# The first group's triangular inverse: substitution on blocks of 16 rows, joined to 32 on TensorE

## The chip, the cores and the metric

One NeuronCore of one Trainium2 chip runs the whole kernel. The metric is the device time of one launch in microseconds (us), the median of several launches. Of each kernel one launch was also taken with the profiler, and all views below come from such launches. All launches quoted were in the fast state: none took over 1.5% more than the fastest of its kernel. A record is one matmul (with its weight load) as the trace lists it; a small fp32 product of the program comes as two of them. A view numbers the lines of the kernel that it was taken from, so the same code has another L number before and after.

## The reference, cut to what matters

```python
def _attn_ref(q, k, v, beta):            # 4 batches x 8 heads, 768 steps, head_dim 48
    k_n = k / (np.linalg.norm(k, axis=-1, keepdims=True) + 1e-06)
    state = np.zeros((B, H, D, D)); y = np.zeros_like(q)
    for t in range(S):
        y[:, :, t] = q_t @ state
        state += beta_t * outer(k_t, v_t - state^T k_t)
def _moe_ref(x, w_gate, w_val, w_out):   # 3072 tokens, 384 -> 1536 -> 384
    g = x @ w_gate
    return (g * sigmoid(g) * (x @ w_val)) @ w_out
# reference: _moe_ref on the attention's y, reshaped to (3072, 384); all fp32 results,
# the weights arrive as 64-bit floats
```

The kernel computes the recurrence in 12 chunks of 64 steps. For each chunk and head it needs the inverse of a 64 x 64 unit triangular matrix. Chunks are inverted in groups of two. The inverses of a group's 32-row diagonal blocks are found by substitution on VectorE, for all heads at once, and TensorE joins two of them to 64 rows. Then come the products of the recurrence (called p_r, p_u, p_s, p_y below), the transposition p_f, and for each chunk the FFN (gate and value products in twelve column tiles, taken in pairs, then the output products p_o).

## The kernel before

The substitution on 32 rows works on all 128 partitions, one 32-row block each, in 31 steps of two instructions:

```python
def substitute(mb, zb):
    for j in range(R - 1):                      # R = 32
        m = R - 1 - j
        ...
        nc.vector.tensor_tensor(out=t_v, in0=zb[:, 0:j+1, j:j+1]..., in1=mb[:, j:j+1, j+1:R]..., op=ALU.mult)
        nc.vector.tensor_tensor(out=zb[:, 0:j+1, j+1:R], in0=zb[...], in1=t_v, op=ALU.add)
```

The start of the program (cut): chunk 0 is joined before the first gate product; chunk 1's join is put behind gate pairs that are already running.

```python
for n, _ in enumerate(substitute(mb, zb)):
    ...                                   # 24 us on VectorE
m_1 = turned_m(1, "ffn")                  # second group's matrix, turned on TensorE meanwhile
...
first_join = join_late(0, 0, ("px", "py"))
next(first_join); converts(2); next(first_q); next(first_join)
step("advance", advance, 0); converts(2)  # chunk 0's recurrence between weight conversions
...
second = join_late(0, 1, ("ffn", "py"))   # chunk 1: handed to the gate loop
first.extend((state_and_join, second_join, lambda: gram(1, True)))
pairs = [(c, f) for c in range(2) for f in range(0, 8, 2)]
```

`converts(n)` turns n pieces of the 64-bit weights into fp32 on VectorE (with some help of ScalarE). `fill` is called in every gate pair and gives VectorE one or two more pieces while there are any, then steps of the second group's inverse.

Of the kernel before, what the change touches and what calls it, by code (L numbers as in the profile page):

```python
# [14 lines left out]
C = 64  # L15
DP = 64
R = 32
PIECE = 512


@with_exitstack
def kernel(
# [8 lines left out]
    moe_w_out: bass.AP,  # L31
    out: bass.AP,
):



# [88 lines left out]
    def load_q(c):  # L125
        for bp in range(NB):
            for b in range(2):
                nc.sync.dma_start(
                    out=qpad[c % QB][64 * b : 64 * b + 64, bp, :, 0:D],
                    in_=halves(q, c, bp, b).rearrange("h p d -> p h d"),  # L130
                )
# [54 lines left out]
    N_HALF = sum(piece[4] < PIECE for piece in pieces)  # L186
    for t in range(FT):
        pieces.append((wo_sb, moe_w_out, t, 0, DM))
    assert DFF == 1536 and KT == 3 and DM <= PIECE and 2 * HH * C == 4 * PIECE

    staged, powers, places = {}, {}, {}

    def words(tile_):
        return tile_.bitcast(U32)
# [30 lines left out]
    def stage(n):  # L225
# [10 lines left out]
            out=place, in_=src[t * 128 : (t + 1) * 128, f0 : f0 + m].bitcast(U32)  # L236
        )

    def power_step(n):
        if n in powers or n not in staged:  # L240
            return
        m = pieces[n][4]
        power = words(hp[10 + (n // 2 % 4 if n < N_HALF else (0, 2, 3, 1)[n % 4])])
        power = power[:, n % 2 * m : n % 2 * m + m] if n < N_HALF else power[:, 0:m]
        powers[n] = power
        nc.vector.tensor_scalar(  # L246
            out=power,
            in0=staged[n][:, :, 1],
            scalar1=0x7FF00000,
            scalar2=None,  # L250
            op0=ALU.bitwise_and,
        )

        nc.scalar.activation(  # L254
            power.bitcast(I32), power, ACTF.Relu, bias=rebias, scale=8.0
        )

    def convert(ns):

        work_of = []  # L260
        for n in ns:
            dst, _, t, f0, m = pieces[n]
            power_step(n)
            work_of.append((dst[:, t, f0 : f0 + m], staged.pop(n), powers.pop(n)))
        for dst, words, _ in work_of:
            nc.vector.tensor_scalar(
                out=dst.bitcast(U32),
                in0=words[:, :, 1],
                scalar1=0xFFFFF,
                scalar2=1 << 20,  # L270
                op0=ALU.bitwise_and,
                op1=ALU.bitwise_or,
            )
        for dst, words, _ in work_of:
            nc.vector.scalar_tensor_tensor(
                out=dst,
                in0=words[:, :, 0],
                scalar=2.0**-32,
                in1=dst.bitcast(U32),
                op0=ALU.mult,  # L280
                op1=ALU.add,
            )
        for n in range(ns[-1] + 1, ns[-1] + 7):
            if n < min(N_HALF, len(pieces)) or ns[-1] + 3 > n < len(pieces):
                power_step(n)
        for _, words, power in work_of:
            nc.vector.scalar_tensor_tensor(
                out=power,
                in0=words[:, :, 1],
                scalar=0x80000000,  # L290
                in1=power,
                op0=ALU.bitwise_and,
                op1=ALU.bitwise_or,
            )
        for dst, _, power in work_of:
            nc.vector.scalar_tensor_tensor(
                out=dst,
                in0=dst,
                scalar=2.0**-20,
                in1=power.bitcast(FP32),  # L300
                op0=ALU.mult,
                op1=ALU.mult,
            )
        for n in ns:
            for later in freed_by.get(n, ()):
                stage(later)
# [10 lines left out]
    for b in range(2):  # L317
        rows = mask_q[64 * b : 64 * b + 64]
        nc.gpsimd.affine_select(
            out=rows,  # L320
            in_=rows,
            compare_op=ALU.is_ge,
            fill=0.0,
            base=-1,
            pattern=[[1, C]],
            channel_multiplier=-1,
        )

    state = const.tile([128, 2, NB, NJ, D], FP32, name="state")
    kt, qt, a_sb, a_of, p_sb, xts = {}, {}, {}, {}, {}, {}  # L330
# [3 lines left out]
    def half_of(x):  # L334
        return slice(64 * x, 64 * x + 64)
# [102 lines left out]
    def gram_steps(c, of_q, tag=None, copies=(nc.vector.tensor_copy,) * 2):  # L438
# [10 lines left out]
        if of_q:  # L449
            p_sb[c] = work.tile([128, 2, NB, NJ, C], FP32, name="p_sb", bufs=2)  # L450
        elif c % 2 == 0:
            a = work.tile([128, C * 2 * HH], FP32, name="a_sb")

            a_sb[c // 2] = (
                a.rearrange("p (i c h) -> p c h i", c=2, h=HH)
                if c == 0
                else a.rearrange("p (c h i) -> p c h i", c=2, h=HH)
            )
            a_of[c // 2] = a
        yield  # L460
        for par in range(2):
# [13 lines left out]
    def gram(*args):  # L475
        for _ in gram_steps(*args):
            pass
# [32 lines left out]
    def substitute(mb, zb):  # L510
        for j in range(R - 1):
# [14 lines left out]
            )  # L526
            yield

    def recur(p, m=D):
        p = p[:, :, 0 : NB * NJ * m]  # L530
        return p.rearrange("p x (bp j d) -> p x bp j d", bp=NB, j=NJ)

    QUADS = [(slice(R * n, R * n + R), R * (n % 2)) for n in range(4)]
    z_late = {}

    def turned_m(g, tag):
# [256 lines left out]
    def gate_val(c, f, fill, within=None):  # L793

        ps = {}
        for w_sb, name in ((wg_sb, "p_gate"), (wv_sb, "p_val")):
# [10 lines left out]
            if name == "p_gate":  # L807
# [3 lines left out]
                if within is not None:  # L811
                    point(within)
        at = len(hs) if c < 2 else (len(hs) - 12) % 8
        hs[c, f] = hp[at].rearrange("p (i n) -> p i n", i=2)
        nc.vector.tensor_tensor(out=hs[c, f], in0=sil, in1=ps["p_val"], op=ALU.mult)  # L815
        if c >= FAST:
# [270 lines left out]
    with tc.manual_schedule(  # L1087
# [13 lines left out]

        nc.vector.memset(places[0][:, 0:1], 0)
        norms(1)
        for n in range(4):
            stage(n)
        load_q(0)
        load_k(2)
        load_k(3)
        for n in range(4, 10):
            stage(n)  # L1110
        load_v(0)
        load_q(1)
        stage(10)
        stage(11)
        copy_a, copy_v = nc.scalar.copy, nc.vector.tensor_copy
        turned(0, False)
        turned(1, False, "py")
        gram(0, False)
        gram(1, False, "py", (copy_a, copy_v))
        mb = new_mb()  # L1120
        a_v = a_of[0].rearrange("p (i m) -> p i m", i=C)
        for _ in turn(
            lambda rows, half: mb[rows],
            lambda rows, half: a_v[rows, R * half : R * half + R],
        ):
            pass
        r_b = first_n()
        copy_v(beta_b, beta_s.rearrange("p (g r) -> p g r", g=NG)[:, :, 0:R])
        for n in range(12, 17):
            stage(n)  # L1130
        load_v(1)
        divide_beta(0, r_b)
        zb = scale_m(mb, [(slice(0, R), mb)], beta_b[:, 0])
        nc.gpsimd.memset(ztp[0], 0.0)

        turned(0, True, "ffn")
        turned(2, False, "px")
        turned(3, False, "py")
        first_q = gram_steps(0, True, "ffn")
        next(first_q)  # L1140
        gram(2, False, "px", (copy_a, copy_a))
        gram(3, False, "py", (copy_a, copy_a))
        for n, _ in enumerate(substitute(mb, zb)):
            if n == R // 2:
                for i in range(4):
                    power_step(i)
        m_1 = turned_m(1, "ffn")
        scale_v_heads(0)
        turned(1, True, "px")
        for _ in late_z(0, zb):  # L1150
            pass
        mb = new_mb()
        mbs.append(mb)
        first_join = join_late(0, 0, ("px", "py"))
        next(first_join)
        converts(2)
        next(first_q)
        next(first_join)
        nc.scalar.copy(mb[:, m_1[0][0]], m_1[0][1])
        step("advance", advance, 0)  # L1160
        converts(2)
        step("advance", advance, 0)
        nc.scalar.copy(mb[:, m_1[1][0]], m_1[1][1])
        converts(2)
        step("advance", advance, 0)
        converts(2)
        step("advance", advance, 0)
        converts(2)
        second_inverse.append(invert(1))
        for _ in range(2):  # L1170
            next(second_inverse[0])
        second = join_late(0, 1, ("ffn", "py"))
        converts(2)

        def state_and_join():
            step("advance", advance, 0)
            next(second)

        def second_join():
            next(second)  # L1180
            gens["join", (0,)] = [None, 2]

        first.extend((state_and_join, second_join, lambda: gram(1, True)))


        pairs = [(c, f) for c in range(2) for f in range(0, 8, 2)]
        pairs += [(c, f) for f in range(8, FT, 2) for c in range(2)]
        for c, f in pairs:
            early = c == 0 and f < 8
            if c == 1 and f == 0:  # L1190
                finish(1)
            elif f > 0:
                point(1 if early else 2)
            need((6, 12, 18, 18, 24, 24)[f // 2])
            gate_val(c, f, fill, 1 if early else None)
# [53 lines left out]
```

## Time and profile before

Times of the kernel before in this study: 748.54 us median beside the changed kernel (747.8 to 749.3 in the other batches). I divide the span at three moments that each trace shows: T, the first gate product; V, the end of the last value product of chunks 0 and 1; G, the first gate product of chunk 2.

The windows view of the kernel before, cut at T, V and G. Columns: start and end, length, busy time and count of TensorE, of weight load, VectorE, ScalarE, GpSimd, then granted clock, DMA share and GB/s.

```profile
0.00:67.57 67.57, 34.41 (x951) 28.94 (x951) 56.56 (x150) 27.81 (x66) 21.49 (x29) 0.71 0.67 159
67.57:155.66 88.09, 87.38 (x1150) 75.74 (x1151) 75.31 (x157) 33.77 (x58) 16.50 (x6) 0.95 0.42 110
155.66:200.58 44.92, 44.23 (x679) 29.19 (x678) 36.41 (x76) 8.48 (x16) 7.34 (x3) 1.00 0.18 33
200.58:748.40 547.82, 540.64 (x7226) 480.23 (x7226) 306.92 (x599) 79.49 (x139) 22.04 (x9) 1.00 0.17 28
```

Length minus TensorE's busy time is its idle time: 33.2 us before T, then only 0.7, 0.7 and 7.2 us. What makes T earlier pays, as long as nothing is added behind it.

From the timeline of TensorE before G: recurrent products of chunk 2 stand between output products (p_o).

```profile
188.12 1.15 PE L695 MATMUL p_r<-state,kt 64*64 64x48 f32 x64
190.26 1.56 PE L829 MATMUL p_o<-wo_sb,h_f 128*128 128x384 f32 x4
...
200.58 2.86 PE L800 MATMUL p_gate<-x_ffn,wg_sb 128*128 128x256 f32 x12 [0.61 <-ACT x_ffn L783]
```

The reader is to see that a set of 64 small records takes 1.15 us here, at full clock, and that large products lie between the sets.

The page's line of the engines and of the queue that brings instructions (packets, MB, share):

```profile
PE 706.7 (94%) x10004; PEld 614.1 (82%) x10004; DVE 475.2 (63%) x981; ACT 149.5 (20%) x277; POOL 67.4 (9%) x46
...
q8 instruction: 78, 1.28, 0.7%
```

It looks like nothing: 0.7%. It turns out to matter, and the prediction did not read it.

### The profile page before, as it was taken

How to read it: one execution, taken by the hardware profiler on the slowest of the kernel's cores; microseconds unless marked ns; L12 is line 12 of the kernel's file. 1: busy time of each engine (PE TensorE's matmuls, PEld its weight loads, DVE VectorE, ACT ScalarE, POOL GpSimd, SP SyncE). 2: the span in 40 equal slices, each digit the busy share in tenths (PEclk: the TensorE clock that was granted, in tenths of full speed). 3: DMA queues.
4: the chain of work that ended last, by engine and by line, in shares of the span. 5: the costliest groups of instructions: out<-in, count | busy, mean ns of one | idle time of the engine just before them, and what ended most of it. 6: DMA issues, size and time to landing. Idle time of an engine off the chain costs nothing.

```text
span 748.4 us, 22217 instructions
## 1 busy us (share of the span) xinstructions
PE 706.7 (94%) x10004; PEld 614.1 (82%) x10004; DVE 475.2 (63%) x981; ACT 149.5 (20%) x277; POOL 67.4 (9%) x46
## 2 busy tenths in 40 slices
PE   4647999999999999999999999999999999999997
PEld 3536888866788688988888988988988988989987
DVE  5899888979368453478863478863478854223122
ACT  2346434211311111112011112011112011021010
POOL 7106200200300000030000030000030000000000
PEclk9755999999999999999999999999999999999999
DMA  7774534230203002231300331401220200000000
GB/s 154 184 213 109 148 68 124 64 53 23 55 14 50 16 16 32 47 61 34 54 14 17 49 61 28 57 10 24 42 46 2 43 3 3 22 3 0 22 1 21
DMA packets 130734, 37.17 MB, mean 50 GB/s; under 512 B 122864, under 2 KB 125936, under 8 KB 130640
## 3 DMA queue, kind: packets, MB, share of 16 engines
q1 hardware_dynamic: 127184, 34.01, 22.4%
q10 hardware_dynamic: 3072, 1.57, 1.0%
q8 instruction: 78, 1.28, 0.7%
q0 software_dynamic: 384, 0.17, 0.2%
q14 instruction: 16, 0.13, 0.1%
HBM read 31.01 MB, written 4.72 MB: 48 GB/s over the span
## 4 chain that ended last, share of the span: by engine, by line
PE 84%; DVE 10%; DMA 1%; issue 1%; SPq 1%; ACT 1%; ACTq 0%; DVEq 0%
PE p_gate L800 24%; PE p_val L800 23%; PE p_o L912 15%; PE p_o L829 6%; DVE tmp L515 3%; DVE zb L521 3%; PE p_g L444 2%; PE p_j L580 2%; PE p_y L735 2%; PE p_u L716 2%; PE p_s L747 2%; PE p_r L695 1%; PE p_y L704 1%; DVE h_f L870 1%; SPq L120 1%
## 5 line engine op out<-in xcount | busy, mean ns | idle before, releaser
L800 PE MATMUL p_gate<-x_ffn,wg_sb 128*128 128x256 f32 x864 | 208.3, 392 | 1.6 <-ACT x_ffn L783 1.6
L800 PE MATMUL p_val<-x_ffn,wv_sb 128*128 128x256 f32 x864 | 198.5, 379 | 0.0
L800 PEld LDWEIGHTS p_gate<-x_ffn,wg_sb 128*128 128x128 f32 x864 | 163.8, 194 | 25.4 <-ACT x_ffn L783 2.1
L800 PEld LDWEIGHTS p_val<-x_ffn,wv_sb 128*128 128x128 f32 x864 | 163.8, 190 | 22.3
L815 DVE TENSOR_TENSOR h_f<-sil,p_val 128x512 f32<-128x512 f32 x71 | 48.5, 684 | 152.4 <-PE p_val L800 151.9
L809 ACT ACTIVATE sil<-p_gate 128x512 f32<-128x512 f32 x72 | 43.0, 598 | 281.7 <-PE p_gate L800 258.1
L608 POOL TENSOR_TENSOR n_b<-mb,half 128x32 f32<-128x32 f32 x5 | 42.2, 8435 | 411.1 <-DVE mb L485 373.3
L912 PE MATMUL p_o<-wo_sb,h_f 128*128 128x192 f32 x432 | 75.6, 328 | 0.1
L515 DVE TENSOR_TENSOR tmp<-zb,mb 128x31 f32<-128x31 f32 (+15 forms) x186 | 63.2, 340 | 16.2 <-PE p_j L580 10.9
L912 PEld LDWEIGHTS p_o<-wo_sb,h_f 128*128 128x128 f32 x432 | 70.3, 190 | 1.2 <-DVE o_sb L922 0.7
L521 DVE TENSOR_TENSOR zb<-zb,tmp 128x31 f32<-128x31 f32 (+15 forms) x186 | 63.7, 342 | 6.4
L922 DVE TENSOR_TENSOR o_sb<-o_sb,p_o 128x192 f32<-128x192 f32 x45 | 15.7, 350 | 53.7 <-PE p_o L912 36.5
L829 PE MATMUL p_o<-wo_sb,h_f 128*128 128x384 f32 x136 | 45.7, 490 | 0.0
L829 PEld LDWEIGHTS p_o<-wo_sb,h_f 128*128 128x128 f32 x136 | 25.4, 190 | 16.5
L912 PE MATMUL p_o<-last_k,h_f 128*128 128x192 f32 x180 | 32.2, 326 | 0.0
L912 PEld LDWEIGHTS p_o<-last_k,h_f 128*128 128x128 f32 x180 | 29.7, 190 | 0.0
L870 DVE TENSOR_TENSOR h_f<-h_f,h_f 128x256 f32<-128x256 f32 x54 | 22.4, 424 | 8.0 <-PE p_o L912 7.1
L912 PE MATMUL p_o<-last_h,h_f 128*128 128x192 f32 x144 | 26.3, 326 | 0.0
L912 PEld LDWEIGHTS p_o<-last_h,h_f 128*128 128x128 f32 x144 | 23.9, 190 | 0.0
L254 ACT ACTIVATE last_h<-last_h,rebias 128x512 int32<-128x512 uint32 (+2 forms) x26 | 15.3, 616 | 31.8 <-DVE last_h L246 31.8
L485 DVE STREAM_TRANSPOSE mb<-a_sb 32x1024 f32<-32x1024 f32 x10 | 19.5, 1949 | 0.3
L716 PEld LDWEIGHTS p_u<-vin,zt 64*64 64x64 f32 x768 | 13.4, 141 | 6.1 <-issue 3.2
(163 smaller groups left out, 677.1 us busy)
## 6 DMA issues: line engine op xcount, KB each, us to landing
vin<-in_v_dram SPq DMA_DIRECT2D x96, 48.0 KB
kn<-in_k_dram SPq DMA_DIRECT2D x40, 96.0 KB
out_dram<-o_sb SPq DMA_DIRECT2D x36, 96.0 KB
zt<-in_moe_w_out_dram SPq DMA_DIRECT2D x6, 384.0 KB
staged<-in_moe_w_out_dram SPq DMA_DIRECT2D x6, 384.0 KB
qpad<-in_q_dram SPq DMA_DIRECT2D x36, 64.0 KB
wo_sb<-in_moe_w_gate_dram SPq DMA_DIRECT2D x4, 512.0 KB
wo_sb<-in_moe_w_val_dram SPq DMA_DIRECT2D x4, 512.0 KB
```

Of the source, the lines that this page charges most:

```text
L485: nc.vector.transpose(out(rows, 0), in_(rows, 0))
L515: nc.vector.tensor_tensor(out=t_v, in0=zb[:, 0 : j + 1, j : j + 1].to_broadcast([128, j + 1, m]), in1=mb[:, j : j + 1, j + 1 : R].to_broad ...
L521: nc.vector.tensor_tensor(out=zb[:, 0 : j + 1, j + 1 : R], in0=zb[:, 0 : j + 1, j + 1 : R], in1=t_v, op=ALU.add,)
L608: nc.gpsimd.tensor_tensor(out=n, in0=mb.rearrange("p j i -> p (j i)")[:, 0 : R * R : R + 1], in1=half, op=ALU.pow,)
L716: nc.tensor.matmul(p_u[half_of(b), par, bp, j], zt[half_of(b ^ par), par, bp, j], r[half_of(b ^ par), par, bp, j], start=first, stop=True, ...
L800: nc.tensor.matmul(ps[name][:, i], w_sb[:, t, (f + i) * 128 : (f + i + 1) * 128], xts[c][:, t], start=(t == 0), stop=(t == KT - 1),)
L809: nc.scalar.activation(sil, ps[name], ACTF.Silu)
L815: nc.vector.tensor_tensor(out=hs[c, f], in0=sil, in1=ps["p_val"], op=ALU.mult)
L829: nc.tensor.matmul(p_o, hs[c, f - f % 2][:, f % 2, bp * 128 : (bp + 1) * 128], wo_sb[:, f], start=(f == 0), stop=(f == FT - 1),)
L870: nc.vector.tensor_tensor(out=out, in0=a, in1=b, op=ALU.subtract)
L912: nc.tensor.matmul(p[x, part], a(f - f % 2)[:, f % 2], b(f), start=not begun and f == 0, stop=f == FH - 1, skip_group_check=True,)
L922: nc.vector.tensor_tensor(out=out, in0=a, in1=b, op=ALU.add)
```

## The change

Its intent is to shorten the 24 us of substitution, in which TensorE mostly waits. Only the first group is changed. The two 16-row diagonal halves of each 32-row block are substituted side by side in one partition (15 steps instead of 31), from grams computed as blocks of their own; the off-diagonal 16 x 16 part follows by products on TensorE. Core of the diff, cut:

```diff
+    def first_gram(c, tag, copies):           # 64 products per chunk, 64x32 tiles
+            nc.tensor.matmul(p_v[hi, par, 1, h], k_v[:, 0], k_v[:, 0])
+            nc.tensor.matmul(p_v[lo, par, :, h], k_v[:, 1], k_v)
+    def first_substitute(m, z):               # RH = 16: two blocks to a partition
+        for j in range(RH - 1):
+            ...
+    def first_m_z(c):                         # 64 products on four quadrants
+                nc.tensor.matmul(p[quad, h], fg.m_up[quad, h], fg.d[quad, :, HH * c + h])
+    def first_rest(p): ...                    # VectorE: identity minus that
+    def first_zt(c, p, blk): ...              # 32 products on two quadrants, twice
+    def first_z(c, p): ...                    # 32 products
+    def first_m_zt(c, p): ...                 # the join to 64 rows: 32 products
+    def first_last(p, t2): ...                # and 32 more
-        for n, _ in enumerate(substitute(mb, zb)):
+        for n, _ in enumerate(first_substitute(m, z)):
-        first_join = join_late(0, 0, ("px", "py"))
...
+        first_turned()
+        p_mz = first_m_z(0)
+        first_rest(p_mz)
+        first_zt(0, p_z[:, 0], 1)
+        first_to(0, p_z[:, 0], both, 1, R)    # copies, ScalarE and VectorE
+        first_zt(0, p_z[:, 0], 0)
+        first_z(0, p_z[:, 1])
+        ...                                   # the same for chunk 1, all ahead of the first gate
-        second = join_late(0, 1, ("ffn", "py"))
-        pairs = [(c, f) for c in range(2) for f in range(0, 8, 2)]
+        pairs = [(c, f + i) for f in (0, 4) for c in range(2) for i in (0, 2)]
         for c, f in pairs:
-            early = c == 0 and f < 8
+            early = c == 0 and f < 4
             if c == 1 and f == 0:
                 finish(1)
+                first.extend((lambda: second_gram(2), lambda: second_gram(3), second_m))
```

So the second group's grams and the turning of its matrix (p_m, 256 records) also leave the head and go into the FFN. The loads of v, q and weights are issued in another order.

## The prediction

> **What bounds the kernel now.** I read the windows by stage first (where TensorE is idle and at what clock), then the timeline of the first 110 us, then the waits of TensorE. The windows, with busy time of TensorE, weight load, VectorE, ScalarE, GpSimd, then the clock:
>
> ```profile
> 0.00:23.63 23.63, 12.83 (x168) 9.79 (x168) 14.79 (x25) 6.90 (x11) 15.35 (x28) 0.93 0.78 157
> 23.63:47.74 24.11, 9.65 (x459) 8.48 (x456) 21.94 (x66) 9.48 (x28) 0.52 (x1) 0.66 0.81 231
> 47.74:67.57 19.83, 11.94 (x327) 10.66 (x327) 19.83 (x59) 11.43 (x27) 5.62 (x1) 0.50 0.36 74
> 67.57:108.25 40.68, 39.97 (x743) 34.08 (x744) 35.17 (x67) 17.59 (x29) 11.73 (x1) 0.90 0.48 128
> 108.25:748.40 640.15, 632.28 (x8312) 551.09 (x8311) 383.47 (x765) 104.15 (x183) 34.16 (x17) 1.00 0.18 33
> ```
>
> The reader is to see a head of 67.57 us in which TensorE is not the bound, and 681 us in which it is busy 98 to 99%. So a gain is an earlier first FFN product, provided no new holes open behind it. In the head VectorE substitutes for 24.1 us (23.63 to 47.74), then 19.8 us of joins and chunk 0 follow. The timeline shows the pieces I use:
>
> ```profile
> 23.63 0.19 DVE L515 TENSOR_TENSOR tmp<-zb,mb 128x31 f32<-128x31 f32 x1
> 34.84 0.42 DVE L515 TENSOR_TENSOR tmp<-zb,mb 128x256 f32<-128x256 f32 x1
> 47.42 0.21 DVE L521 TENSOR_TENSOR zb<-zb,tmp 128x31 f32<-128x31 f32 x1
> 33.52 2.07 PE L544 MATMUL p_m<-ident,a_sb 32*32 32x32 f32 x128 [0.54 <-issue]
> 61.05 1.96 PE L735 MATMUL p_y<-uu,p_sb 64*64 64x48 f32 x64 [0.69 <-ACT uu L727]
> 67.57 5.28 PE L800 MATMUL p_gate<-x_ffn,wg_sb 128*128 128x256 f32 x12 [0.95 <-ACT x_ffn L783]
> 73.86 2.00 PE L568 MATMUL p_j<-zt,a_sb 32*32 32x32 f32 x64
> 182.88 2.00 PE L580 MATMUL p_j<-ident,d_t 32*32 32x32 f32 x64
> 180.26 1.20 PE L568 MATMUL p_j<-zt,a_sb 32*32 32x32 f32 x64
> ```
>
> A substitution step costs 0.19 us for 31 elements and 0.42 for 256; start to start it fits 0.195 us + elements/960 us per instruction. A small product comes as two records. On two quadrants with a strided operand a record takes 31 ns (2.00/64), on four 16 ns (2.07/128), on two with both operands contiguous 19 ns (1.20/64). The first gate product takes 5.28 us, later ones 2.59 start to start. The second thing to see is that VectorE is nearly full too from 47.7 to 108 (55.0 of 60.5 us): it converts weights, 2.8 us for two pieces of 256 columns, 2.5 us for one of 512. TensorE hardly waits because 12 pieces are done when its first product starts.
>
> **What the Trainium skill says.** "TensorE: Matmul & The Clock Gate", section "What's actually happening": the array's clock is halved by default and only sustained activity releases it. The trace agrees: 0.50 in the third window, 5.28 against 2.59 us. "TensorEngine Tiling (Array Packing)", section "Key Properties": tiles load and multiply independently; agrees (31 ns on two quadrants, 16 on four). "SBUF — State Buffer", section "Door 1: The DMA port swizzle", note on cachelines: reading a new 16-byte line for each element costs extra. The trace agrees for the stationary operand: L580 (stride of 32 floats) takes 2.00 us also at full clock, L568 falls to 1.20 when group 1 stores its operand contiguously. That a strided moving operand is as slow no row here shows; I assume it.
>
> **The change, part by part.**
>
> Start of the substitution. The first grams become 64 products per chunk instead of 32. Before, 128 records took 3.69 us; now 256, by dispatch (16 ns) 4.1 us, by the row halves up to 6.8: end at about 16 us. Copies of half size 0.6, norm, reciprocal and transposition 0.8, one transposition 1.27 in place of three (1.25 + 2.48), scaling 0.95 with half the elements: start at about 19.8 instead of 23.63.
>
> Substitution. 15 steps of two instructions, elements 2(j+1)(15-j), together 1360 per instruction kind: 30 x 0.195 + 2 x 1360/960 = 8.7 us, and two exponent steps 0.4: 9.1 instead of 24.1. End S at 28.9 instead of 47.7, 18.8 us earlier.
>
> Joins. What follows is now a chain on TensorE. From S: transposition 1.2; 64 products on four quadrants 2.07 (to 3.4); subtraction 0.7 (4.2); three sets of 32 products on two quadrants, 31 ns x 192 = 5.95 (10.2); the next product set on contiguous operands about 1.4, its copy 0.6, then a ScalarE copy of the upper part 0.4 that stands in the way of chunk 1's first 64 products (2.07): 14.8; chunk 0's last set 1.4; chunk 1's first set 2.0; p_u 2.0 (half clock, as p_y's 1.96), then, in TensorE's order ahead of p_y, two more sets 4.0; p_y 2.0; six copies of y 1.96; p_f 1.55; eight transpositions of q 1.95; and the last set 1.4, which waits for ScalarE's copies behind x_ffn. With 0.05 to 0.15 us per handover this adds to 33.3 us, where the old kernel needs 19.8, because both chunks' joins now lie ahead of the first gate. First gate T at 28.9 + 33.3 = 62.2 instead of 67.57: gain 5.4 us of the 18.8.
>
> Behind the first gate. VectorE has converted only 6 pieces at T (old: 10 to 12), as it waited for the joins. The new order of pairs (chunk 0, columns 0 and 2, then chunk 1) needs 12 pieces, and needs chunk 1's attention after two pairs, not four. From the order of instructions: piece 7 waits for ScalarE until T + 1.7; then VectorE stands until the first value product ends at T + 5.3 + 1.1 + 2.6 = T + 9; then product 0.7, pieces 9 and 10 2.4, mask 1.35, pieces 11 and 12 with exponents 4.35, pieces 13 and 14 4.9, and only then the two operations on v (2.05): p_u starts at T + 24.8. TensorE has nothing between the second value product (ends T + 19) and p_u: a hole of about 6 us. After it p_u, copy 0.85, p_s and p_y, copies 1.45, p_f, copy 0.8 run with no gates between them: 7.2 us at full clock, 10.4 at half; mean 8.8, gate of chunk 1 at T + 33.6. The old kernel takes 40.7 from T to that gate, with two more pairs (10.4) and a join (1.93 + 3.75 = 5.7) in it, so 24.6 for the same work: loss 9.0.
>
> Moved TensorE work: in the FFN -5.7 (join), +2.2 (grams of chunks 2, 3), +4.1 (256 records of p_m): +0.6. Clock: the gate after p_m at half clock +1.6 (old: 4.19 us after the join at 206, for 2.59), the gate after the hole +1.5.
>
> End of the first two chunks. The second inverse is emitted wholly after the last gate pair, and its join and chunk 2 stand in one block after all output products, where the old kernel has them between. The inverse itself (about 31 us) is covered by the 33 us of output products. But t, zt copies (2.34), p_r, p_u, uu, p_y, y, p_f run serially: about 49 us from last value product to the next gate at full clock, 53 at half, against 46.8 for the old (44.8, plus 2.0 for a transposition and a gram done earlier there): loss 2 to 6, say 4.
>
> Sum: -5.4 + 9.0 + 0.6 + 3.1 + 4 = +11.3 us. The clock terms (3.1, 1.6 in the mean of the advance, 2 in the last) may be absent; counting half of them takes off 3.3. Result 747.7 + 8 = about 756 us.
>
> **The rivals.**
> 1. The gain of the head is kept. The substitution falls by 15 us, and TensorE bounds all the rest; if small sets run at 19 ns, not 31 (strided moving operand not slow), four sets lose 0.8 each, T is at 59, and if the holes are covered too, the time is 738 to 742. For it: TensorE waits only 1.6 us for x_ffn in the whole trace. Against it: VectorE's 55 of 60.5 us, the instruction order.
> 2. VectorE becomes the bound behind the gate, as above, but the clock also stays at half through the joins of p_m and of the second group: 762 to 767.
> 3. Transfers: weights and v are issued in another order, v ahead of most weights. Pieces 2 to 8 are issued by about 30 us and needed after 49; the DMA share of 0.36 in the third window speaks against a wait. 0 us. If beta landed only near 20 us, the substitution would start some 2 us later.
>
> **Range and chances.** Head: T 59 to 65 (3 us either way); hole and serial chunk 1: 5 to 11; end 0 to 8; clock 0 to 4. Combined: 741 to 767. Faster by over 2% is below 732.7, which needs the whole head saving and no loss: 0.05. Slower by over 2% is above 762.7: 0.18. Within: 0.77.
>
> **What would show it.** Substitution about 9 us long, ending near 29; first gate at 59 to 65 at half clock; TensorE idle about 6 us before chunk 1's p_u with VectorE at weights; 64-record sets at 2 us; the second join after all output products. It is wrong if VectorE delivers v before the second value product ends, if the first gate lies before 55, or if no hole over 2 us shows between 62 and 100 us.

## The result, and the profile after

The changed kernel took 775.53 us (774.69 to 778.79, 4 launches); the kernel before, in the same rounds, 748.54. The ratio is 1.0373, interval 1.0333 to 1.0413. It is slower by 3.7%, above the predicted range. Ratios here are the mean time of one kernel's fast runs over that of the other's of the same rounds, so not quite the ratio of the medians.

The windows of the changed kernel, cut at the start and end of the substitution and at T, V and G (columns as before):

```profile
0.00:21.11 21.11, 10.45 (x285) 8.04 (x286) 11.79 (x21) 9.31 (x16) 17.54 (x31) 0.95 0.69 132
21.11:30.04 8.93, 4.59 (x76) 3.83 (x75) 7.96 (x32) 5.58 (x18) 0.00 (x0) 0.69 0.63 151
30.04:69.07 39.03, 29.34 (x1038) 27.65 (x1039) 22.48 (x53) 13.57 (x32) 0.00 (x0) 0.53 0.71 184
69.07:170.69 101.62, 89.62 (x1274) 76.77 (x1271) 73.83 (x152) 34.44 (x60) 7.24 (x2) 0.90 0.30 86
170.69:224.62 53.93, 50.80 (x751) 36.41 (x749) 42.17 (x93) 11.17 (x20) 10.28 (x7) 0.84 0.25 43
224.62:773.80 549.18, 541.86 (x7230) 481.22 (x7226) 309.17 (x607) 79.57 (x139) 22.03 (x9) 0.99 0.16 27
```

The substitution is 8.93 us long, 15.2 less than before. But T is 1.5 us later. The span grew by 25.4 us: 1.5 before T, 13.5 from T to V, 9.0 from V to G, 1.4 behind G. From T to G TensorE stood 15.1 us idle (1.4 before) and was busy 8.8 us longer.

Where the head lost what the substitution gave, in TensorE's timeline (start, length, operation, in brackets the idle time before it and what ended it):

```profile
37.85 2.01 PE L670 MATMUL p_z<-once 32*32 32x32 f32 x64 [1.45 <-DVE zt L696]
48.65 0.44 PE L654 MATMUL p_mz<-d_t,once 32*32 32x32 f32 x17 [2.19 <-issue]
53.75 0.67 PE L670 MATMUL p_z<-once 32*32 32x32 f32 x17 [1.80 <-issue]
69.07 2.86 PE L982 MATMUL p_gate<-x_ffn,wg_sb 128*128 128x256 f32 x12
```

Two things were not in the prediction. TensorE waits 1.45 us for a copy of half a tile, because ScalarE's half (0.58 us from 36.49) and VectorE's (0.70 us from 37.10) ran one after the other. And 4.0 us are "issue": TensorE waits for nothing that the profile can name. Between the two gaps lie exactly 128 records.

Behind T, TensorE waits for chunk 1's v, in the timelines of TensorE and of VectorE:

```profile
91.49 1.96 PE L898 MATMUL p_u<-vin,zt 64*64 64x48 f32 x64 [5.49 <-DVE vin L894]
```
```profile
89.43 0.95 DVE L423 TENSOR_TENSOR vin<-vin,n_t 128x768 f32<-128x768 f32 x1
...
110.74 0.69 DVE L998 TENSOR_TENSOR h_f<-sil,p_val 128x512 f32<-128x512 f32 x1 [10.11 <-PE p_val L982]
```

This is the predicted hole: VectorE was at weights until 89.43, then at the scaling and subtraction on v. And from 100.6 us on VectorE itself stands still for 10.11 us: it seems not to have been short of time, only in the wrong order (e9 tests this).

At the end of the first two chunks the recurrent products no longer have large ones between them:

```profile
208.95 1.96 PE L877 MATMUL p_r<-state,kt 64*64 64x48 f32 x64
...
224.62 4.19 PE L982 MATMUL p_gate<-x_ffn,wg_sb 128*128 128x256 f32 x12
```

1.96 for 1.15 us: half clock. The gate after them pays as well, 4.19 for 2.86.

The page of the changed kernel, the lines shown of before:

```profile
PE 726.7 (94%) x10644; PEld 633.9 (82%) x10644; DVE 467.4 (60%) x956; ACT 153.6 (20%) x284; POOL 57.1 (7%) x49
...
q8 instruction: 83, 1.36, 0.7%
```

TensorE's records grew by 640 and the instruction queue's packets by 5: 128 records to a packet, and a packet is 1.36 MB / 83 = 16 KB. The gaps marked issue lie one packet apart.

### The profile page after: what moved, and what is told of

It reads as the page before. It is cut to its first block, busy times and chain, and to the rows that moved or that the text cites. A ratio compares the mean times of both kernels' runs of the same rounds, so it can differ in the third digit from the quotient of the medians.

```text
span 773.8 us, 23488 instructions
## 1 busy us (share of the span) xinstructions
PE 726.7 (94%) x10644; PEld 633.9 (82%) x10644; DVE 467.4 (60%) x956; ACT 153.6 (20%) x284; POOL 57.1 (7%) x49
## 3 DMA queue, kind: packets, MB, share of 16 engines
q8 instruction: 83, 1.36, 0.7%
## 4 chain that ended last, share of the span: by engine, by line
PE 63%; DVE 7%; issue 1%; ACT 1%; DMA 1%; DVEq 0%
PE p_gate L982 19%; PE p_val L982 18%; PE p_o L1095 13%; PE p_o L1012 2%; DVE tmp L532 2%; PE p_u L898 1%; PE p_g L466 1%; DVE zb L538 1%; PE p_s L929 1%; PE p_y L886 1%; PE p_y L917 1%; PE p_r L877 1%; DVE h_f L1053 1%; DVE h_f L998 1%; PE p_f L962 1%
## 5 line engine op out<-in xcount | busy, mean ns | idle before, releaser
L790 POOL TENSOR_TENSOR n_b<-mb,half 128x32 f32<-128x32 f32 x5 | 30.3, 6052 | 479.1 <-DVE mb L502 369.0
L532 DVE TENSOR_TENSOR tmp<-zb,mb 128x31 f32<-128x31 f32 (+15 forms) x155 | 52.7, 340 | 7.4 <-PE p_j L762 3.1
L538 DVE TENSOR_TENSOR zb<-zb,tmp 128x31 f32<-128x31 f32 (+15 forms) x155 | 53.1, 343 | 5.3
L1053 DVE TENSOR_TENSOR h_f<-h_f,h_f 128x256 f32<-128x256 f32 x54 | 22.4, 424 | 8.0 <-PE p_o L1095 7.1
L262 ACT ACTIVATE last_h<-last_h,rebias 128x384 int32<-128x384 uint32 (+2 forms) x28 | 16.8, 617 | 41.6 <-DVE last_h L254 41.5
L898 PE MATMUL p_u<-vin,zt 64*64 64x48 f32 x768 | 16.2, 241 | 5.5 <-DVE vin L894 5.5
```

The lines of the kernel that those rows point to most:

```text
L262: nc.scalar.activation(power.bitcast(I32), power, ACTF.Relu, bias=rebias, scale=8.0)
L532: nc.vector.tensor_tensor(out=t_v, in0=zb[:, 0 : j + 1, j : j + 1].to_broadcast([128, j + 1, m]), in1=mb[:, j : j + 1, j + 1 : R].to_broad ...
L538: nc.vector.tensor_tensor(out=zb[:, 0 : j + 1, j + 1 : R], in0=zb[:, 0 : j + 1, j + 1 : R], in1=t_v, op=ALU.add,)
L790: nc.gpsimd.tensor_tensor(out=n, in0=mb.rearrange("p j i -> p (j i)")[:, 0 : R * R : R + 1], in1=half, op=ALU.pow,)
L898: nc.tensor.matmul(p_u[half_of(b), par, bp, j], zt[half_of(b ^ par), par, bp, j], r[half_of(b ^ par), par, bp, j], start=first, stop=True, ...
L1053: nc.vector.tensor_tensor(out=out, in0=a, in1=b, op=ALU.subtract)
```

## The experiments

Twelve kernels ran; all gave the correct result. In this table, "gaps" is the idle time of TensorE marked issue from 30 us to the first gate ("hidden": during the old substitution, when TensorE mostly waits), and T, T to chunk 1's first gate, and T to G are from the one profiled launch of each.

| run | median us | ratio to before | T | gaps | T to chunk 1's gate | T to G |
|---|---|---|---|---|---|---|
| before | 748.5 | 1 | 67.57 | 4.2 (3.0 hidden) | 40.5 (other work in it) | 133.0 |
| changed | 775.5 | 1.037 | 69.07 | 4.0 | 33.5 | 155.6 |
| e1 old pairs | 771.1 | 1.030 | 69.14 | 4.1 | (other work in it) | 152.1 |
| e2 zero fills | 774.3 | 1.034 | 68.70 | 6.2 | 33.5 | 155.7 |
| e3 late loads | 773.9 | 1.032 | 70.52 | 5.5 | 33.5 | 155.4 |
| e4 fills | 767.9 | 1.025 | 68.80 | 4.0 | 32.9 | 147.9 |
| e5 join behind | 770.8 | 1.030 | 58.39 | 0.9 | (other work in it) | 159.4 |
| e6 several | 770.8 | 1.029 | 59.85 | 4.4 | (other work in it) | 160.0 |
| e7 quiet | 771.9 | 1.030 | 66.30 | 1.3 | 33.5 | 155.5 |
| e8 e6 + fills | 789.7 | 1.054 | 58.96 | 2.4 | (other work in it) | 167.6 |
| e9 hold | 771.9 | 1.032 | 72.33 | 6.3 | 26.8 | 150.8 |
| e10 four quadrants | 775.6 | 1.036 | 71.21 | 8.1 | 34.3 | 153.3 |
| e11 all repairs | 754.5 | 1.008 | 65.46 | 5.6 | 25.3 | 140.6 |
| e12 padding | 776.0 | 1.038 | 74.41 | 9.7 | 32.9 | 148.9 |

The intervals of the ratios are 0.002 to 0.005 wide to each side. The changed kernel was timed in the first batch only, and the medians of the kernel before differ by up to 1.5 us from batch to batch, so that a total within some 2 us of 775.5 (e2, e3, e10, e12) shows neither gain nor loss. The changed kernel, e1, e4 and e9 have the same head; their gaps (4.0, 4.1, 4.0, 6.3) and T (68.8 to 72.3) show how much single launches scatter.

### e1: the old order of gate pairs

```diff
-        pairs = [(c, f + i) for f in (0, 4) for c in range(2) for i in (0, 2)]
+        pairs = [(c, f) for c in range(2) for f in range(0, 8, 2)]
-            early = c == 0 and f < 4
+            early = c == 0 and f < 8
```

> The changed kernel with the old order of the gate pairs (four pairs of chunk 0, then chunk 1). Theory A, the new order of the pairs is what costs: it leaves chunk 1's attention with nothing beside it, so with the old order the hole of 5.5 us before chunk 1's p_u and its serial steps (8.9 us together against the old kernel) go away and the time falls by 7 to 10 us, to about 767. Rival B, VectorE is late with the weights because the joins held it, and any order waits for VectorE: the hole before p_u becomes a wait of the third gate pair on wg_sb or wv_sb of 6 to 12 us, and the time stays within 3 us of the changed kernel's 775.5.

Measured 771.08 (769.0 to 773.55), 4.4 below the changed kernel. The sum lies between the two expectations, and the trace shows that it comes from elsewhere than I had thought. TensorE's timeline, inside chunk 0's third gate product, after the first 4 of its 12 records:

```profile
99.23 3.78 PE L982 MATMUL p_gate<-x_ffn,wg_sb 128*128 128x256 f32 x8 [3.71 <-DVE wg_sb L305]
```

The hole of 5.49 us ahead of p_u is still there (at 91.56), and this second one, for weights, has joined it. T to V did not gain (102.5 for 101.6). V to G did, 49.5 for 53.9, because the second group's inverse ended sooner (the transposition of its result began at 197.8, in the changed kernel at 202.6). So the pair order as such is not the cause of the hole; e9 looks for it elsewhere.

### e2: zero fills on VectorE

```diff
-        nc.gpsimd.memset(fg.m_up, 0.0)
+        nc.vector.memset(fg.m_up, 0.0)
-        nc.gpsimd.memset(ztp[0], 0.0)         # before the substitution
+        nc.vector.memset(ztp[0], 0.0)         # earlier, between the two grams
```

> The changed kernel with GpSimd's two zero fills of the head (zt, 2048 elements, and once, 512) done by VectorE while it waits for the first grams. Theory: two VectorE tensor-scalar instructions (0.92 us and 1.72 us instead of 0.18 us each) were held up by GpSimd's fills that ran beside them, so nb falls back to 0.2 us, the substitution starts 1.5 to 2.2 us earlier (21.1 to about 19.2) and the first gate comes as much earlier, total about 773.5. Rival: these two waited for something else (the beta products); then the start of the substitution stays within 0.4 us.

In the changed kernel two tensor-scalar instructions of VectorE, on 32 elements, lay beside long zero fills of GpSimd. One of them there, and then the same one here, in VectorE's timeline:

```profile
18.56 1.72 DVE L609 TENSOR_SCALAR nb<-beta_b 128x32 f32<-128x32 f32 x1
```
```profile
17.75 0.14 DVE L609 TENSOR_SCALAR nb<-beta_b 128x32 f32<-128x32 f32 x1
```

1.72 against 0.14 us; the fill beside the first ran from 18.44 for 1.80 us, so they end within 0.04 us. The Trainium skill, "SBUF — State Buffer", section "Who interferes with whom", says that copies and tensor-scalar operations can, with suitable operands, take a port pair that VectorE shares with GpSimd, and that whoever comes second is blocked for a whole instruction; this pair of lines agrees. The substitution began at 18.72 instead of 21.11, 2.4 us sooner. But T was 68.70, 0.4 sooner, and the total 774.27 (772.03 to 775.78): the gaps marked issue had grown from 4.0 to 6.2. A true repair of the start, of which the first gate kept little.

### e3: five weight loads issued behind the join

```diff
         scale_v_heads(0)
-        for n in range(12, 17):
-            stage(n)
...
         gens["join", (0,)] = [None, 2]
+        for n in range(12, 17):
+            stage(n)
         load_v(1)
```

> The changed kernel with five weight loads (2.3 MB) issued after chunk 0's join instead of ahead of it. TensorE stood twice for 'issue' inside a run of small products (2.2 us at 46.5 and 1.8 us at 51.9), each time after 128 of them. Theory: its instructions are fetched in blocks of that size and the fetch queues behind the weight loads (DMA share 0.92 there): the gaps shrink to below 1 us each and the first gate comes 2 to 3 us earlier. Rival: the gap is the fetch's own latency, whatever the load: the gaps stay within 0.5 us and the time within 1 us, unless the later loads cost a wait of VectorE.

Measured 773.92 (769.93 to 776.82). (The five loads are of 512 KB each, some 2.5 MB; the 2.3 above is a slip.) The issue order alone delayed the transfers by about 10 us. The windows from 40 to 60 us in steps of 10, first of the changed kernel, then of this one:

```profile
40.00:50.00 10.00, 6.50 (x294) 6.12 (x291) 2.19 (x4) 2.24 (x4) 0.00 (x0) 0.50 0.98 290
50.00:60.00 10.00, 8.12 (x282) 7.70 (x279) 6.73 (x17) 2.74 (x6) 0.00 (x0) 0.50 0.40 91
```
```profile
40.00:50.00 10.00, 8.25 (x361) 7.85 (x358) 3.44 (x5) 2.82 (x5) 0.00 (x0) 0.50 0.53 93
50.00:60.00 10.00, 5.56 (x184) 5.26 (x183) 5.28 (x15) 2.17 (x5) 0.00 (x0) 0.50 0.93 317
```

Where the DMA share fell from 0.98 to 0.53, TensorE did 361 records for 294 and had no gap marked issue until 49.5 us; where it rose from 0.40 to 0.93, it did 184 for 282, with gaps of 1.25 and 3.64 us (at 50.8 and 58.5). The gaps follow the weight transfers. T was not better (70.52), since the transfers only moved to another part of the same chain.

The Trainium skill, "Runtime: NRT & Kernel Launch", section "Instruction fetch mechanics", describes what is at work: an engine's instructions are brought in blocks of 16 KiB, 256 instructions, by DMA, while it works on the block before. One record of a small product is a weight load and a matmul, two instructions, so a block is 128 records: the counts on the two pages, and the 128 records between gaps, agree. The page calls the cost mostly hidden; here it is not.

### e7: no weight transfer while the chain runs

```diff
+        if hold:                              # in stage(): a one-column write first
+            nc.scalar.copy(place[:, 0:1].bitcast(FP32), half[:, 0:1])
         nc.sync.dma_start(out=place, ...)
...
-        for n in range(12, 17): stage(n)      # ahead of the chain
+        for n in range(12, 17): stage(n, True)  # ScalarE comes to it at the first gate
```

> The changed kernel with five weight loads (2.5 MB) held back until ScalarE has come to the first gate, so no bulk transfer runs between about 42 us and the first gate, but for chunk 1's v. Theory: TensorE's gaps that the trace marks as issue come at every 128th record of small products, which is one 16 KB packet of the instruction queue, and are that packet's delay behind the weight transfers. So gaps between 40 us and the first gate fall from 4.0 us to under 1, and the first gate comes at 65 to 66.5 us; total 768 to 773 unless the late weights hold VectorE up. Rival: the gaps are fixed costs of TensorE's own sequencer at these places: gaps of 3 us or more remain and the first gate stays at 68.5 to 69.5 us.

From TensorE's timeline of this run:

```profile
51.24 0.66 PE L672 MATMUL p_z<-once 32*32 32x32 f32 x17 [0.98 <-issue]
```

With one of 0.36 at 43.24 the gaps came to 1.3 us in all (a little over the 1 us that I had expected), at packet boundaries still, and T came at 66.30, 2.8 us sooner. The total was 771.93 (767.14 to 774.78). From T to G nothing changed (155.5), so the late weights cost nothing. The rival, a cost that does not depend on the transfers, falls for most of the gap time, but not for all of it. In the FFN of the changed kernel stands this line of TensorE's timeline:

```profile
127.44 1.62 PE L726 MATMUL p_m<-ident,a_sb 32*32 32x32 f32 x98 [1.47 <-issue]
```

The DMA share from 122.60 to 127.44 is 0.02, and yet there is a gap; it is 1.61 us in e7 and 1.33 in e11. The packed traces keep the time of every instruction packet, though no view lists them one by one, and they settle the matter. Each of the 40 gaps in the table above ends 1.2 to 1.7 us after an instruction packet has landed, and all stand at the same place of a block of 128 records. What varies is when that packet starts, counted from the first record of the block before: 0.6 to 0.8 us in the p_m of four runs, with no other transfer, but 3.6 us at the gap of 2.19 in the changed kernel and 6.5 us at the gap of 4.06 in e12, with the DMA engines full. The packet's own transfer takes 0.9 to 1.7 us in either case. So the transfers delay the start of the packet, and there is a floor as well: with idle DMA engines one block followed the other after 3.0 to 3.6 us at best where TensorE had to wait for it, and the 128 records of p_m, on four quadrants, need only about 2.0.

### e12: 128 more records where TensorE is idle

```diff
-        for bp, j, par, b, _ in every():
+        for bp, j, par, b, _ in list(every()) * times:
...
-        first_q = gram_steps(0, True, "ffn")
+        first_q = gram_steps(0, True, "ffn", times=3)
```

> The changed kernel, with the 64 products of chunk 0's q gram issued three times instead of once (same result): 128 more records, one packet of the instruction queue, put where TensorE stands idle for 5.75 us before the chain. Theory: the chain is held by the supply of instruction packets behind the weight transfers, one for each 128 records every 5 to 6 us, so an idle TensorE does not make the records free: the gaps marked issue in the head grow by 3 to 6 us, the first gate comes 3 to 6 us later, total 778 to 782. Rival: TensorE's own time and its waits set the chain, 4 us of work in an idle stretch of 5.75 cost nothing: gaps and first gate as in the changed kernel (69 to 70), total within 1 us of 775.5.

From TensorE's timeline of this run, ahead of the first gate:

```profile
37.10 0.44 PE L654 MATMUL p_mz<-d_t,once 32*32 32x32 f32 x16 [4.06 <-issue]
50.47 0.64 PE L682 MATMUL p_j<-zt,a_sb 32*32 32x32 f32 x17 [3.64 <-issue]
```

In the head this is what the theory of the packets said: work put wholly into idle time made the chain later, with gaps of 9.7 us (a third one is 2.00, at 59.30) against 4.0, and T at 74.41, 5.3 us later, outside the scatter of the four equal heads. But the total, expected at 778 to 782, was 775.97 (774.93 to 777.32), no more than the changed kernel's. T to G was 148.9, 6.6 us less. Most of it is the clock of the last block, here in the same timeline:

```profile
212.10 1.15 PE L877 MATMUL p_r<-state,kt 64*64 64x48 f32 x64
```

1.15 us where the changed kernel needs 1.96, with the same code in the same order: here the granted clock stayed full until 223.6 us, there it was halved from 206.9. From V to G it makes 49.5 us here and 53.9 there; the prediction had 49 at full clock and 53 at half. So the totals of kernels with such a block carry some 4 us that depend on when the clock switches. What decides that moment is open, and I saw it in one launch of this kernel only. It is why I judge single repairs by their stage in the trace, not by the total.

### e4: the second group's inverse drawn forward

```diff
-            converts(2 if len(filled) < 4 else 1)
+            converts(2 if len(filled) < 4 or 6 < len(filled) < 13 else 1)
```

> The changed kernel, but fill steps 7 to 12 convert two weight pieces each instead of one. VectorE stands 10 us at 100 to 110, so these fit. Theory: the second group's inverse comes late (its 31 us start only after the last gate pair) because the last weight piece is emitted there; with conversions ended some 3 pairs earlier the inverse starts in the gates, the joins lie between the output products again, and the stretch from the last value product to chunk 2's first gate falls from 53.9 to 46 to 49 us: total 768 to 771. Rival: the inverse waits on something else (GpSimd's power, transfers of the last pieces), or the gates now wait for weights; total within 2 us of 775.5.

From TensorE's timeline of this run, ahead of chunk 2's first gate:

```profile
205.79 1.56 PE L1012 MATMUL p_o<-wo_sb,h_f 128*128 128x384 f32 x4
207.27 1.15 PE L898 MATMUL p_u<-vin,zt 64*64 64x48 f32 x64
```

Measured 767.86 (766.16 to 768.48); chunk 2's first gate is at 216.72, not 224.62. With the weights converted sooner the second inverse starts sooner (the transposition of its result at 190.4, not 202.6), its join and the recurrent products stand between output products again, and T to G is 7.6 us shorter. The end of the first two chunks lost what it lost because this inverse came too late.

### e9: chunk 1's v ahead of further weights

```diff
-            gate_val(c, f, fill, 1 if early else None)
+            gate_val(c, f, (lambda n: None) if (c, f) == (0, 2) else fill, 1 if early else None)
```

> The changed kernel, with one thing else: behind chunk 0's second gate pair VectorE converts no further weights, so that the scaling and subtraction on chunk 1's v follow directly behind the weights of that pair. The old order of pairs did not take the hole away (5.5 us before chunk 1's first product, and 3.7 more at a gate), so its cause is not the pair order as such. Theory: it is VectorE's order of work, v behind two more pieces of 512 columns (4.9 us) and the gated product of the second pair. Then the hole before chunk 1's first product falls from 5.5 to under 1 us, the first gate of chunk 1 comes 5 to 7 us sooner after the first gate of chunk 0 (26.5 to 28.5 instead of 33.5), and the total is 768 to 771. Rival: VectorE's whole backlog is the bound; the two pieces held back are then missed at the next pairs, TensorE waits there for weights, and the total stays at 773 or more.

Chunk 1's first product in TensorE's timeline of this run:

```profile
91.61 1.15 PE L898 MATMUL p_u<-vin,zt 64*64 64x48 f32 x64 [0.54 <-DVE vin L894]
```

The hole went from 5.49 to 0.54 us, p_u ran at full clock (1.15 for 1.96), and chunk 1's first gate came at 99.16, 26.8 us after T instead of 33.5. No wait for weights took its place, so the rival falls: the cause is the order on VectorE. The total, 771.92 (771.33 to 774.17), lies just above what I expected: in the profiled launch T happened to be at 72.33, by gaps of 6.3 us, and 2.7 us came back as a wait for a transposed k behind V.

### e5, e6 and e8: chunk 1's join behind the gate

e5 has the old order of pairs and emits chunk 1's whole join after the first gate pairs:

```diff
-        p_mz = first_m_z(1)
-        first_rest(p_mz)
...
+        first.extend((state_mz, zt_1, m_zt_1, last_1, lambda: gram(1, True)))
```

> The changed kernel, with the old order of gate pairs and with all of chunk 1's join of the first group (the product of off-diagonal block and second inverse, and its three product sets after it) placed behind the first gate pairs. Theory now: the time from the substitution's end to the first gate is the number of small products ahead of that gate, at about 4 us for 128 records at half clock and 5.3 to 5.9 us where TensorE also stands between blocks of 128 records. 384 records leave the head, so the first gate falls from 69.1 to 55 to 58 us. They cost 10 to 11 us again behind the gate, plus half clock in the gates after them (up to 6). Total 762 to 772. Rival: VectorE bounds the stage behind the first gate, so an earlier first gate is worth nothing: first gate at 55 to 58 all the same, TensorE idle over 8 us more before 110, total 771 or more.

T came at 58.39, 10.7 us sooner: fewer records ahead of it. But T to G took 159.4, and the total was 770.79 (769.18 to 772.97), inside the expected range, near its upper end. TensorE waited 5.7 us there for weights (ended by VectorE), and gates behind the small sets ran at half clock. A join is not free by being moved.

e6 adds the four-quadrant product set, copies on ScalarE alone, conversions spread through the head, zero fills on VectorE, and has chunk 1's off-diagonal product in the head again.

```diff
+        first_zt4(0, p_z[:, 0])               # four quadrants once
+        first_to(0, p_z[:, 0], (copy_a, copy_a), 1, R)
+        converts(2)                           # at three more places in the chain
```

> As the run with chunk 1's join behind, and besides: the product set of each chunk that used two quadrants twice now uses four quadrants once, all copies of the chain are on ScalarE so that VectorE converts weights meanwhile, conversions are spread through the head, zero fills are on VectorE, and the off-diagonal product of chunk 1 is back in the head. If the serial copies (1.45 us of TensorE's wait and 2 us of products) and the conversions that VectorE missed while it served the chain are the loss, the first gate comes at 51 to 55 us, TensorE has no hole over 3 us between there and 100 us, total 755 to 764. Rival: ScalarE now carries the chain and x_ffn both, the first gate does not come before 57 and the total stays at 764 or more.

From TensorE's timeline of this run, behind the first gate:

```profile
73.21 2.02 PE L676 MATMUL p_z<-once 32*32 32x32 f32 x128 [7.17 <-ACT state L946]
```

770.78 (768.08 to 771.46), the rival. T was 59.85, and a new wait of 7.17 us stood behind the first gate: ScalarE came to the copy of the state only after exponents of weights that VectorE had handed to it. I had moved work from one in-order engine to another.

e8 is e6 with e4's fills:

> The version with all the repairs of the head, plus two pieces for each fill in fills 7 to 12 as in the run that drew the second group's inverse forward. If the two losses are independent, this is 7 to 8 us below the version without the fills: 747 to 757. Rival: the second inverse drawn forward collides with the chunk 1 join that now lies behind the gate, and the gain is under 3 us.

789.72 (788.15 to 791.21): neither expectation. T to G grew to 167.6 (with a wait of 9.43 us for ScalarE's copy of the state behind the first gate, and one of 5.05 for its x_ffn before chunk 1's gate), and 562.9 us passed behind G, where e6 needs 548.7; waits for v, for the gated product and for x_ffn appear there. Which order on VectorE leads to them I did not follow up. This combination was left.

### e10: four quadrants once

```diff
-        first_zt(0, p_z[:, 0], 1)
+        first_zt4(0, p_z[:, 0])
         first_to(0, p_z[:, 0], both, 1, R)
-        first_zt(0, p_z[:, 0], 0)
```

(and the same for chunk 1)

> The changed kernel, with each chunk's first 16 by 32 product set done on four quadrants once (64 records pairs at 16 ns) where the change uses two quadrants twice at 31 ns with a copy between. Theory: the serial copies of the two halves, for which TensorE waits 1.45 us, and the second set of 2.0 us leave the chain in chunk 0, and 2.0 us in chunk 1: the first gate comes 3.5 to 5.5 us sooner (63.5 to 65.5), total 770 to 772. Rival: the chain is then held by the next thing, the instruction packets behind the weight transfers, and more time is lost between blocks of 128 records: the first gate gains under 2 us.

From TensorE's timeline of this run, in the chain:

```profile
58.99 0.77 PE L904 MATMUL p_u<-vin,zt 64*64 64x48 f32 x17 [1.91 <-issue]
```

775.59 (774.31 to 776.1), no gain, as the rival said; T was 71.21 with gaps of 8.1 us, one of them in this line. One set on four quadrants is faster on the array than two on two, but it is the same 128 records, the same packet. The wait for the two serial copies was not removed either: it is 1.48 us here, at 40.08, ahead of the next set.

### e11: the repairs together

e4's fills, e7's held loads, e2's zero fills, e9's order and e10's product set in one kernel.

> The changed kernel with five repairs at once: two pieces for each fill in fills 7 to 12, five weight loads held back until the first gate, zero fills on VectorE, no conversion behind chunk 0's second pair, and the four-quadrant product set. If the single gains add (7.7 by the fills, 3.6 by the loads, 1.3 by the zero fills, and expected 5.5 by the order of v and 4.5 by the product set), 750 to 756. It should stay above the kernel before, because 2 us of grams, the transposition of the second group's matrix (5.5 us) and the half clock behind it stay in the FFN. Rival: the gains overlap on VectorE's backlog, 757 to 765.

The windows of this run from T to V and from V to G:

```profile
65.46:159.75 94.29, 87.88 (x1347) 75.16 (x1343) 79.26 (x175) 37.10 (x70) 15.23 (x6) 0.96 0.45 129
159.75:206.02 46.27, 45.46 (x679) 29.61 (x677) 36.50 (x76) 8.46 (x16) 7.34 (x3) 0.96 0.21 37
```

754.47 (752.01 to 758.39, 5 launches), ratio 1.0082 (1.0044 to 1.012), inside the expected 750 to 756 and 21 us below the changed kernel. That it fell there is partly luck: the expectation counted 5.5 us for the order of v and 4.5 for the product set, which alone gave 3.6 and 0. The single gains in the medians (7.7, 3.6, 1.3, 3.6 and 0) add to 16; together they gave 5 more. The gaps did not fall to those of e7: they are 5.6 us, of which 2.94 stand in the four-quadrant set at 37.08, as in e6, e8 and e10 (1.49 to 3.49 there). Transfers issued earlier, which this run does not hold back, still fill the DMA engines then (share 1.02 from 35 to 40 us). T is 2.1 us earlier than in the kernel before, and TensorE's idle time from T to G is 7.2 us instead of 15.1. It is less than 1% slower than the kernel before, but clear of the noise: T to G is 140.6 against 133.0, of which 5.8 are more idle time, most of it at chunk 1's serial products, at one wait for weights and at a packet gap in p_m. No version here beats the kernel before.

## Why the prediction was wrong

By its own steps; times are from the profiled launches, in which the span grew by 25.4 us.

| step of the prediction | predicted | measured |
|---|---|---|
| start of the substitution | 19.8 | 21.11 |
| its length | 9.1 | 8.93 |
| from its end S to the first gate | 33.3 | 39.0 |
| first gate T against before | −5.4 | +1.5 |
| T to chunk 1's first gate; loss against the prediction's 24.6 | 33.6; +9.0 | 33.5; +8.9 |
| work moved into the FFN | +0.6 | +2.0 |
| half clock in the FFN | +3.1 | +4.2 |
| end of the first two chunks | +4 | +7.0 |
| behind G | 0 | +1.4 |
| taken off, half of the clock terms | −3.3 | none |
| sum | +8 | +25 |

**Right.** The substitution's cost, the hole for chunk 1's v with its engine and nearly its length (5.5 for "about 6 us"), and the shape of the end.

**Right by luck.** The time to chunk 1's gate came within 0.1, by two errors that cancel: the first gate was forecast at half clock (5.3 us) and ran at full clock (2.86), so that p_u began at T + 22.4 and not at T + 24.8, and from p_u to the gate it took 11.1 us where the forecast had 8.8.

**The step that failed** is "With 0.05 to 0.15 us per handover this adds to 33.3 us" and, from it, "T at 28.9 + 33.3 = 62.2". The chain took 39.0. Of the 5.7 us, 4.0 are gaps between instruction packets, which e3, e7 and e12 tie to the weight transfers: less bulk traffic, 1.3; 128 records more, 9.7. Another 1.45 are a wait for the copies of two halves, run in turn, which the sum did not have between the sets at all; and chunk 0's two sets on contiguous operands took 1.9 us each at half clock where I had put about 1.4. That is a little more than 5.7; other terms came out smaller. The handovers were short-changed too: the terms alone add to 32.65, which leaves 0.65 us for 16 of them. The start was 1.3 us late, from tensor-scalar instructions blocked by GpSimd's zero fill (e2: 1.72 against 0.14). The prediction's rival on transfers asked only whether weights would come too late, and gave 0 us. The harm was that they stood in the way of instructions. Of the 17 us between +8 and +25 the head makes 6.9, the clock terms 4.4, the end 3.0, p_m 1.4 and the part behind G 1.4.

What was exchanged: the substitution gave 15.2 us on VectorE, and 951 records of TensorE before T became 1398, at mean clock 0.53 behind the substitution, in a chain in which nearly every product waits for the one before. e11, repaired as far as was tried, has T at 65.46, 2.1 us of gain, with gaps of 5.6 us still in it; without them T would be near 60 (an estimate from these two numbers). No run shows a head without gaps.

**Terms of the right kind and the wrong size.** The end: the mechanism (join and chunk 2 in one block after the output products) was right, but the upper end of "2 to 6" was passed: 7.0, with nearly the whole block at half clock, from 206.9 us up to the gate (4.19). In e12, with the same block at full clock, V to G took 49.5 us, which is the lower end. e4 shows that the late inverse is the cause, not the products. The clock terms: the prediction halved them as uncertain; they came in full (gate of chunk 1 5.46, gate after p_m 4.21, for 2.75). And p_m took 5.5 us instead of 4.1, with one more packet gap (1.47) in it, at a DMA share of 0.02.

**What remains open.** When exactly the clock switches in the last block (e12), what fills the 1.2 to 1.7 us from the landing of an instruction packet to TensorE's next record, and why e8 loses 14 us behind G.

## What to carry to other kernels

Count the instructions, not only the array's time: many small fp32 products come as two instructions for each record, and while bulk loads fill the DMA engines their instruction packets arrive late. Even with no transfer beside it, a block of 128 records that ran in 2 us was not followed at once. So look in the timeline for "issue" gaps at equal distances of records and keep heavy transfers out of such stretches. Before taking work from one engine and giving it to another as a chain, add up the new chain at the clock that it will really have. And when an earlier stage frees an engine, read again what stands in that engine's order behind it: one line that put v before two more weights was worth 6.7 us of a stage, of which the total kept 3.6.

## What the Trainium skill lacked or had wrong

- "Runtime: NRT & Kernel Launch", "Instruction fetch mechanics": the block size agrees (640 more records, 5 more packets of 16 KB), but the cost of a block boundary was not mostly hidden. It was 4.0 to 6.3 us before the first gate in four launches of the same head, 1.3 with the five weight loads held back, 9.7 with 128 more records, and 1.47 at one boundary in p_m with the DMA share at 0.02. That bulk transfers delay the fetch is not said there.
- "TensorE: Matmul & The Clock Gate", "What's actually happening": sustained activity is said to release the clock. It did not for streams of small products: in the changed kernel from 54.34 to 64.19 us TensorE was busy 9.77 of 9.85 us at a clock of 0.50, and in e7 from 50 to 60 us busy 9.0 of 10 at 0.50. The page has no word on what small tiles count for.
